# Second batch's exponentials taken slot by slot from PSUM on ScalarE, and wider zeros in the empty products

## The chip, the cores and the metric

The kernel runs on 1 core of one Trainium2 chip. The metric is the device time of one execution in microseconds (us); of several runs the median is given. PE is TensorE (PEld its weight loads), DVE is VectorE, ACT is ScalarE, POOL is GpSimd, SP is SyncE, which here issues DMAs.

## What is computed

Attention over two batches of 8 heads, 576 positions and head size 64. The first four heads see a local window of 32, the last four see every 32nd position. The result goes through a product of two linear maps, two more linear maps, and a mixture of four experts.

```python
scores = scale * np.matmul(q, k.transpose(0, 1, 3, 2))
...
scores = np.where(masks[None, :, :, :], scores, -1000000000.0)
scores = scores - np.max(scores, axis=-1, keepdims=True)
attn = np.exp(scores)
attn = attn / (np.sum(attn, axis=-1, keepdims=True) + 1e-09)
return np.matmul(attn, v).astype(np.float32)
...
a = x @ w1
b = x @ w2
h = a * b @ w3
return (h @ w_out).astype(np.float32)
...
p = domain_probs / (domain_probs.sum(-1, keepdims=True) + 1e-09)
for e in range(E):
    h = np.maximum(x @ w1[e], 0.0)
    out += p[:, e:e + 1] * (h @ w2[e])
```

Only masked-in blocks of the scores are computed. A slot is one such block: 64 columns for a local head, 54 for a strided one.

## The kernel before

**Stages.** Up to about 31 us the attention of the first batch (b = 0) runs alone, while the first weights arrive. From 31 us TensorE works on `x @ w1` and `x @ w2` (`ab_block`, accumulators `ab_acc`), in units of two accumulators, 12 matmuls of 288 columns each; after units 2, 4, 5, 7, 8, 10, 11, 13 and 14 one step of the second batch's attention (`attend(1, s)`, s = 0 to 8) is put between them. This lasts to about 98 us. Then follow the second batch's units, the map `w3 @ w_out`, its product with the former result, and the experts, to the end.

**Everything in full precision is done with split numbers.** A value is kept as a rounded part (`w_hi`, `x_hi`) and a remainder (`w_lo`, `x_lo`), and each product is three (`mm3`, L266 to L268). Making the parts is work for ACT and DVE: for each 1 MB piece of weights ACT runs L143, L151 and the rounding L172, and DVE runs L154, L157, L160, L164 and the remainder L182. `advance()` issues this work piece by piece between the units, so it stands on the same two queues as the attention.

**A step of the attention.** `Chunk4` holds 6 slots (local, g = 0) or 8 (strided, g = 1), six chunks for a batch. `scores` fills one PSUM bank `sc`. `maxima` reduces it to one maximum for each slot (L370) and writes score minus maximum to the tile `p_ring` (L375). `exps` is one ACTIVATE over all slots (L381). One step later `sums` adds up each slot (L390 or L388), adds 1e-9 (L391, g = 0 only; for g = 1 a column of 1e-9 that POOL has written is summed too) and inverts (L392), and `normalise` multiplies (L396, on POOL for b = 0, on DVE for b = 1). Then TensorE transposes (`tp`, L401), ACT copies the result out of PSUM (`pT`, L406), TensorE multiplies with the values (`o`, L418 or L427), ACT takes the rounded part (`x_hi`, L454) and DVE the remainder (`x_lo`, L458).

**Order.** Each engine works off its own instructions in the order in which the code issues them; semaphores make it wait for others. In `attend` that is: scores of s + 1, maxima and exps of s, sums and normalise of s - 1, product with values and rounding of s - 3, transposes and copy of s - 2. So on ACT the copy `pT`, the rounding `x_hi` and the copies `ab` that free TensorE's banks (L503) stand behind the exponentials of the same step. The accumulators `tp`, `o` and `ab_acc` share five PSUM banks (pool `ps`), the scores have three of their own.

**Empty products.** `keep_warm(n)` issues n products of zeros into a spare bank while TensorE would wait. There are 42 in the first 31 us, each 128x512 in bf16 with its own weight load (L119).

Of the kernel before, what the change touches and what calls it, by code (L numbers as in the profile page):

```python
# [8 lines left out]
F32 = mybir.dt.float32  # L9
F32R = mybir.dt.float32r  # L10
BF16 = mybir.dt.bfloat16
I32 = mybir.dt.int32
U32 = mybir.dt.uint32
AF = mybir.ActivationFunctionType
# [4 lines left out]
P = 128  # L19
# [9 lines left out]
NBLK = NT // BLK  # L29
NTT = NT // P  # L30
NEG = -8.0e9
WARM = 7
SCALE = 1.0 / float(D) ** 0.5

EXP_LO, EXP_HI = 3.0517578125e-05, 122880.0
# [7 lines left out]
def kernel(  # L43
# [13 lines left out]
    nc = tc.nc  # L57
    mm = nc.tensor.matmul
# [7 lines left out]
    small = ctx.enter_context(tc.tile_pool(name="small", bufs=4))  # L66
# [5 lines left out]
    def bank(name):  # L72
        return ps.tile([P, 512], F32, tag="ps", name=name)
# [33 lines left out]
    def warm_up():  # L107

        idle = tmp.tile([P, P], F32, tag="pT", name="idle")
        nc.vector.memset(idle, 0.0)  # L110
        nc.scalar.activation(small.tile([P, 1], F32, tag="rec", name="one"), idle[:, :1], AF.Exp)
        zeros = idle.bitcast(BF16)
        moving = zeros.unsqueeze(1).to_broadcast([P, 2, 2 * P])

        def keep_warm(n):
            if n:
                acc = bank("idle")
            for i in range(n):
                mm(acc.rearrange("p (a b) -> p a b", a=2), zeros[:, :P], moving, start=i == 0, stop=i == n - 1)  # L119

        keep_warm(WARM)
        return keep_warm
# [80 lines left out]
    def load_next(held=False):  # L203
        nonlocal loaded
        if loaded < len(stream):
            stream[loaded].raw_load(held)
            loaded += 1
            for load in rest_loads.pop(loaded, ()):
                load()
# [46 lines left out]
    def advance(n=1):  # L256

        return all([next(worker, False) for _ in range(n)])
# [16 lines left out]
    def load_qk(b, g, cut=0, held=False):  # L275

        pair = big[b].tile([P, 2, 2, S], F32, tag="big", name="tqk")
        tq, tk = pair[:, 0], pair[:, 1]
        hold(held, tk[:, 0, :1])
        pairs = slice(2 * g, 2 * g + 2)  # L280
        for c in ([slice(0, cut), slice(cut, S)] if cut else [slice(0, S)]):
            for t, src, queue in ((tk, kT, nc.sync), (tq, qT, nc.scalar if cut else nc.sync)):
                queue.dma_start(out=t[:, :, c], in_=src[b, pairs, :, c].rearrange("k p n -> p k n"))
        qk[b, g] = (tq, tk)
# [36 lines left out]
    class Chunk4:  # L321
# [45 lines left out]
        def maxima(self):  # L367
            s = self.slots
            mx = small.tile([P, 8], F32, tag="mx", name="mx")
            nc.vector.tensor_reduce(out=mx[:, :s], in_=self.sc, axis=mybir.AxisListType.X, op=ALU.max)  # L370
            self.frame = p_ring[self.index % 4]
            self.p = self.frame[:, :s, :self.nk]
            if self.g:
                nc.gpsimd.memset(self.frame[:, :, T3:T3 + 1], 1e-9)
            nc.vector.tensor_tensor(out=self.p, in0=self.sc, in1=self.wide(mx), op=ALU.subtract)  # L375
# [2 lines left out]
            return t[:, :self.slots].unsqueeze(2).to_broadcast([P, self.slots, self.nk])  # L378

        def exps(self):  # L380
            nc.scalar.activation(self.p, self.p, AF.Exp, scale=SCALE)  # L381

        def sums(self):
            s = self.slots
            self.rec = small.tile([P, 8], F32, tag="rec", name="rec")
            rec = self.rec[:, :s]
            if self.g:
                nc.vector.tensor_reduce(out=rec, in_=self.frame[:, :s, :T3 + 1], axis=mybir.AxisListType.X, op=ALU.add)  # L388
            else:
                nc.vector.tensor_reduce(out=rec, in_=self.p, axis=mybir.AxisListType.X, op=ALU.add)  # L390
                nc.vector.tensor_scalar_add(rec, rec, 1e-9)  # L391
            nc.vector.reciprocal(rec, rec)  # L392
# [188 lines left out]
    class Weights:  # L581
# [17 lines left out]
        def work(self):  # L599
# [20 lines left out]
            if self.again:  # L620
                for i, u in enumerate(sums):
                    nc.sync.dma_start(out=u.bitcast(F32), in_=stored[self.at][i])
            else:
                yield from self.split(sums, w)
                for i, u in enumerate(sums):
                    nc.sync.dma_start(out=stored[self.at][i], in_=u.bitcast(F32))
# [120 lines left out]

    with tc.manual_schedule():
        keep_warm = warm_up()
        load_qk(0, 0, CUT)  # L750
        local_masks()
# [63 lines left out]
        first[1].scores()  # L815
        for s in range(9):
            if s == 2:
                keep_warm(6)
                first[3].scores()
            if s == 3:  # L820
                keep_warm(2)
            if 3 <= s:
                first[s - 3].pv()
            if 2 <= s < 8:
                first[s - 2].transposes()
            if s + 1 in (2, 4, 5):
                first[s + 1].scores()
            keep_warm({0: 3, 5: 5, 6: 7, 7: 7, 8: 5}.get(s, 0))
            if s < 6:
                first[s].maxima()  # L830
                first[s].exps()
            if 1 <= s < 7:
                first[s - 1].sums()
                first[s - 1].normalise()
            if s in (3, 4, 6):
                load_next(True)
            if s == 5:
                load_qk(1, 0, held=True)
            if 3 <= s:
                first[s - 3].put()  # L840
                first[s - 3].put_lo()
                if s != 6:
                    live -= 1
            advance({5: 3, 6: 1, 7: 1}.get(s, 0))
            if 2 <= s < 8:
                first[s - 2].evac(nc.scalar.copy)
            if s == 6:
                c_w12[0].round_up()
# [21 lines left out]
        for it in range(8):  # L870
# [8 lines left out]
            i = {1: 0, 3: 1, 6: 2}.get(it)  # L879
# [141 lines left out]
```

## Time and profile before

| | us |
|---|---|
| median of 3 runs | 626.93 (626.92 to 627.87) |
| the profiled execution, its own time | 628.45 |
| its span, first to last instruction | 626.3 |
| PE busy | 615.6 |
| DVE busy | 450.4 |
| ACT busy | 265.0 |
| POOL busy | 10.1 |

The span is what the trace shows; the rest of the execution's own time lies around it. TensorE is busy for 98% of the span, so a wait of TensorE anywhere is a good part of what can be lost or won. A matmul's busy time includes its way through the array, so a few hundred ns of waiting can hide in it: start times tell more than busy shares.

### The profile page before, as it was taken

To read this page: it belongs to the slowest core of one execution; us is meant where nothing else is said; L and a number is where in the kernel's file an instruction comes from. 1 tells how busy PE (TensorE), PEld (TensorE's weight loads), DVE (VectorE), ACT (ScalarE), POOL (GpSimd) and SP (SyncE) were. 2 spreads that over 40 slices of the span, in tenths; PEclk is the share of its full clock that TensorE was granted. 3 is DMA by queue.
4 is the path that set the end of the run, shared out by engine and by line. 5 is a ranking of instruction groups with operands and counts; after the bars stand their busy time and mean duration, and the time that the engine had idled before them with its cause. 6 is when DMAs were issued, how large, how long until landed. Compare 5 with 4: busy or idle time off the path is not lost.

```text
span 626.3 us, 11330 instructions
## 1 busy us (share of the span) xinstructions
PE 615.6 (98%) x4632; PEld 559.5 (89%) x4632; DVE 450.4 (72%) x813; ACT 265.0 (42%) x455; POOL 10.1 (2%) x37
## 2 busy tenths in 40 slices
PE   8899999999999999999999999999999999999997
PEld 5598899999889999999989999899889898989996
DVE  4889995989784224867977888788775665755843
ACT  3564574765654123433343433434433333333320
POOL 4100000000000000000000000000000000000000
PEclk9899999999999999999999999999999999999999
DMA  8876330235522210344344344354586566565411
GB/s 262 291 272 190 127 137 2 92 124 186 205 78 97 95 68 1 135 163 174 135 166 170 136 173 163 135 188 159 196 297 253 181 224 219 186 214 189 154 49 67
DMA packets 28726, 99.43 MB, mean 159 GB/s; under 512 B 2652, under 2 KB 6740, under 8 KB 26116
## 3 DMA queue, kind: packets, MB, share of 16 engines
q1 hardware_dynamic: 28132, 98.14, 44.5%
q8 instruction: 36, 0.59, 0.4%
q10 hardware_dynamic: 544, 0.59, 0.3%
q14 instruction: 14, 0.11, 0.1%
HBM read 79.58 MB, written 19.14 MB: 158 GB/s over the span
## 4 chain that ended last, share of the span: by engine, by line
PE 88%; DVE 4%; DMA 3%; ACT 3%; issue 2%; POOL 0%; SPq 0%; DVEq 0%
PE g_acc L266 11%; PE g_acc L267 11%; PE g_acc L268 10%; PE m_a L268 4%; PE m_a L267 4%; PE m_a L266 4%; PE m_b L267 3%; PE m_c L266 3%; PE x_acc L268 3%; PE x_acc L267 3%; PE x_acc L266 3%; PE m_c L267 3%; PE m_b L266 3%; PE m_c L268 3%; PE m_b L268 3%; PE ab_acc L266 3%
## 5 line engine op out<-in xcount | busy, mean ns | idle before, releaser
L657 ACT ACTIVATE h_hi<-u 128x320 fp32r<-128x320 f32 (+1 forms) x128 | 56.9, 445 | 189.0 <-DVE u L663 189.0
L266 PE MATMUL g_acc<-w_hi,h_hi 128*128 128x512 f32 (+1 forms) x296 | 114.3, 386 | 0.0
L267 PE MATMUL g_acc<-w_lo,h_hi 128*128 128x512 f32 (+1 forms) x296 | 114.2, 386 | 0.0
L268 PE MATMUL g_acc<-w_hi,h_lo 128*128 128x512 f32 (+1 forms) x296 | 113.7, 384 | 0.0
L596 DVE TENSOR_TENSOR w_lo<-raw,w_hi 128x768 fp32r<-128x768 f32 x64 | 69.4, 1084 | 12.4 <-ACT w_hi L594 12.4
L663 DVE TENSOR_TENSOR u<-m_b,u 128x320 f32<-128x320 f32 (+1 forms) x96 | 40.7, 452 | 51.1 <-PE m_b L268 51.1
L266 PE MATMUL ab_acc<-x_hi,w_hi 128*128 128x288 f32 x252 | 75.2, 298 | 1.3 <-ACT pT L406 1.0
L268 PE MATMUL ab_acc<-x_hi,w_lo 128*128 128x288 f32 x252 | 74.2, 294 | 0.0
L267 PE MATMUL ab_acc<-x_lo,w_hi 128*128 128x288 f32 x252 | 74.2, 294 | 0.0
L268 PEld LDWEIGHTS g_acc<-w_hi,h_lo 128*128 128x128 f32 x296 | 55.6, 188 | 11.6
L266 PEld LDWEIGHTS g_acc<-w_hi,h_hi 128*128 128x128 f32 x296 | 55.8, 188 | 8.0
L267 PEld LDWEIGHTS g_acc<-w_lo,h_hi 128*128 128x128 f32 x296 | 55.7, 188 | 7.6
L659 DVE SCALAR_TENSOR_TENSOR h_lo<-u,h_hi 128x320 fp32r<-128x320 f32 (+1 forms) x128 | 57.6, 450 | 3.6 <-ACT h_hi L657 1.8
L594 ACT CAST w_hi<-raw 128x768 fp32r<-128x768 f32 x64 | 59.9, 936 | 0.0
L266 PEld LDWEIGHTS ab_acc<-x_hi,w_hi 128*128 128x128 f32 x252 | 47.3, 188 | 2.0 <-ACT pT L406 1.2
L267 PEld LDWEIGHTS ab_acc<-x_lo,w_hi 128*128 128x128 f32 x252 | 47.3, 188 | 0.0
L268 PEld LDWEIGHTS ab_acc<-x_hi,w_lo 128*128 128x128 f32 x252 | 47.3, 188 | 0.0
L267 PE MATMUL m_b<-b_t,s_hi 128*128 128x320 f32 (+1 forms) x128 | 37.9, 296 | 0.0
L663 DVE TENSOR_TENSOR u<-m_a,u 128x320 f32<-128x320 f32 (+1 forms) x64 | 28.9, 451 | 11.6 <-PE m_a L268 11.6
L596 DVE TENSOR_TENSOR s_lo<-raw,s_hi 128x1024 fp32r<-128x1024 f32 x16 | 19.6, 1225 | 24.3 <-ACT s_hi L594 24.3
L663 DVE TENSOR_TENSOR u<-m_c,u 128x320 f32<-128x320 f32 (+1 forms) x64 | 29.0, 452 | 4.5 <-PE m_c L268 3.9
L673 ACT COPY u<-m_a 128x320 f32<-128x320 f32 (+1 forms) x32 | 12.7, 398 | 42.3 <-PE m_a L268 42.3
(162 smaller groups left out, 1398.2 us busy)
## 6 DMA issues: line engine op xcount, KB each, us to landing
raw<-in_e_dram SPq DMA_DIRECT2D x32, 1024.0 KB, 5.1
raw<-in_w_dram SPq DMA_DIRECT2D x8, 1024.0 KB, 6.4
raw<-in_w3T_dram SPq DMA_DIRECT2D x8, 1024.0 KB, 4.9
stored<-s_hi SPq DMA_DIRECT2D x16, 512.0 KB, 2.6
stored<-s_lo SPq DMA_DIRECT2D x16, 512.0 KB, 2.6
s_hi<-stored SPq DMA_DIRECT2D x16, 512.0 KB, 3.5
s_lo<-stored SPq DMA_DIRECT2D x16, 512.0 KB, 6.9
raw<-in_w_out_dram SPq DMA_DIRECT2D x4, 1024.0 KB, 8.4
```

Of the source, the lines that this page charges most:

```text
L266: mm(acc, lh, rh, start=first, stop=False)
L267: mm(acc, lh, rl, start=False, stop=False)
L268: mm(acc, ll, rh, start=False, stop=last)
L594: nc.scalar.copy(dst[0], src)
L596: nc.vector.tensor_tensor(out=dst[1], in0=src, in1=dst[0].bitcast(F32), op=ALU.subtract)
L657: nc.scalar.activation(hi, src, AF.Relu)
L659: nc.vector.scalar_tensor_tensor(out=lo, in0=src, scalar=0.0, in1=hi.bitcast(F32), op0=ALU.max, op1=ALU.subtract)
L663: nc.vector.tensor_tensor(out=out, in0=acc, in1=b, op=ALU.add)
L673: nc.scalar.copy(u1, a)
```

## The change

In the second batch (b = 1) `maxima` keeps only the reduction; POOL multiplies the maxima by -SCALE. `exps` becomes one ACTIVATE for each slot: it reads the scores from PSUM, takes the scaled maximum as its bias, and writes the sum of its slot (`accum_out`) to `rec`. `sums` shrinks to an addition of 1e-9, on POOL, and the reciprocal on DVE. `keep_warm` multiplies 32-bit zeros, 128x512, instead of bf16, and is called for 10 products instead of 42: 2 for 7 at the start, 1 for 6, 0 for 2, 1 for 3, 1 for 5, 2 for 7 twice, 1 for 5.

```diff
-WARM = 7
+WARM = 2
...
-        zeros = idle.bitcast(BF16)
-        moving = zeros.unsqueeze(1).to_broadcast([P, 2, 2 * P])
+        moving = idle.unsqueeze(1).to_broadcast([P, 4, P])
...
-                mm(acc.rearrange("p (a b) -> p a b", a=2), zeros[:, :P], moving, start=i == 0, stop=i == n - 1)
+                mm(acc.rearrange("p (a b) -> p a b", a=4), idle, moving, start=i == 0, stop=i == n - 1)
...
             self.p = self.frame[:, :s, :self.nk]
+            if self.b:
+                self.mx = mx
+                nc.gpsimd.tensor_scalar_mul(mx[:, :s], mx[:, :s], -SCALE)
+                return
             if self.g:
                 nc.gpsimd.memset(self.frame[:, :, T3:T3 + 1], 1e-9)
             nc.vector.tensor_tensor(out=self.p, in0=self.sc, in1=self.wide(mx), op=ALU.subtract)
...
         def exps(self):
+            if self.b:
+                self.rec = small.tile([P, 8], F32, tag="rec", name="rec")
+                for s in range(self.slots):
+                    at = slice(s, s + 1)
+                    nc.scalar.activation(self.p[:, s], self.sc[:, s], AF.Exp, bias=self.mx[:, at], scale=SCALE,
+                                         accum_out=self.rec[:, at])
+                return
             nc.scalar.activation(self.p, self.p, AF.Exp, scale=SCALE)
...
-            self.rec = small.tile([P, 8], F32, tag="rec", name="rec")
+            if not self.b:
+                self.rec = small.tile([P, 8], F32, tag="rec", name="rec")
             rec = self.rec[:, :s]
-            if self.g:
+            if self.b:
+                nc.gpsimd.tensor_scalar_add(rec, rec, 1e-9)
+            elif self.g:
...
             if s == 2:
-                keep_warm(6)
+                keep_warm(1)
                 first[3].scores()
-            if s == 3:
-                keep_warm(2)
...
-            keep_warm({0: 3, 5: 5, 6: 7, 7: 7, 8: 5}.get(s, 0))
+            keep_warm({0: 1, 5: 1, 6: 2, 7: 2, 8: 1}.get(s, 0))
```

Line numbers in the changed kernel differ by a few: exponentials L381 become L388, maxima L370 become L369, `x_lo` L458 becomes L471.

On DVE, step s = 1 of the second batch stands like this before; `t` and `w_lo` belong to the splitting of weights, `mx` are the maxima, `rec` the sums and their inverses.

```order
L164 ISA t<-raw_621,t 128x2048
L370 TENSOR_REDUCE mx<-sc 128x6
L375 TENSOR_TENSOR p_ring<-sc,mx 128x384
L390 TENSOR_REDUCE rec<-p_ring 128x6
L391 TENSOR_SCALAR rec<-rec 128x6
L392 RECIPROCAL rec<-rec 128x6
L396 TENSOR_TENSOR p_ring<-p_ring,rec 128x384
L154 TENSOR_SCALAR t<-t 128x1024
```

And in the changed kernel, at the same place on DVE:

```order
L163 ISA t<-raw_592,t 128x2048
L369 TENSOR_REDUCE mx<-sc 128x6
L405 RECIPROCAL rec<-rec 128x6
L409 TENSOR_TENSOR p_ring<-p_ring,rec 128x384
L153 TENSOR_SCALAR t<-t 128x1024
```

The subtraction, the sum and the addition have left DVE's row; the reciprocal stands right behind the maxima, and in front of it, on POOL, now stand the scaling of this step's maxima and the addition to the last step's sums, in that order.

On ACT, step s = 3 stands like this before; `x_hi` and `pT` are the attention's, `ab` frees a bank of TensorE, `raw` and `t` are weights.

```order
L381 ACTIVATE p_ring<-p_ring 128x8x54
L454 CAST x_hi<-o 128x2x3x32 x2
L406 COPY pT<-tp 128x384
L503 COPY ab<-ab_acc 128x288
L143 ACTIVATE raw_883<-raw_883 128x1024
```

And in the changed kernel, at the same place on ACT:

```order
L388 ACTIVATE p_ring,rec<-sc,mx 128x54 x8
L467 CAST x_hi<-o 128x2x3x32 x2
L419 COPY pT<-tp 128x384
L516 COPY ab<-ab_acc 128x288
L142 ACTIVATE raw_856<-raw_856 128x1024
```

One exponential has become eight, and the same rounding, copies and weight work stand behind them in the same order.

## Rows read from the trace of the kernel before

**Rows 1.** The page: busy us (share) xinstructions; the chain's shares by engine.

```profile
PE 615.6 (98%) x4632; PEld 559.5 (89%) x4632; DVE 450.4 (72%) x813; ACT 265.0 (42%) x455; POOL 10.1 (2%) x37
...
PE 88%; DVE 4%; DMA 3%; ACT 3%; issue 2%; POOL 0%; SPq 0%; DVEq 0%
```

**Rows 2.** Busy time by stretch: us, PE, PEld, DVE, ACT, POOL, clock, DMA.

```profile
50.00:70.00 20.00, 19.14 (x300) 17.93 (x300) 19.41 (x36) 10.14 (x17) 0.23 (x2) 1.00 0.62 204
```

**Rows 3.** Waits of PE from 30 to 190 us, the longest: total us, times, longest.

```profile
PE ab_acc L266 <- ACT pT L406: 1.0, 1, 1.0
```

**Rows 4.** The chain that ended last, step 0: start us, us, what.

```profile
43.91 0.53 ACT p_ring L381
...
44.72 0.95 ACT w_hi L172
```

**Rows 5.** Timeline of DVE, 42 to 72 us: start us, us, engine, line, operation [idle before].

```profile
42.73 0.55 DVE L370 TENSOR_REDUCE mx<-sc 128x6 f32<-128x384 f32 x1
...
45.70 1.23 DVE L182 TENSOR_TENSOR w_lo<-t,w_hi 128x1024 fp32r<-128x1024 f32 x1 [0.49 <-ACT w_hi L172]
...
53.71 1.21 DVE L182 TENSOR_TENSOR w_lo<-t,w_hi 128x1024 fp32r<-128x1024 f32 x1
...
69.37 0.60 DVE L370 TENSOR_REDUCE mx<-sc 128x8 f32<-128x432 f32 x1
...
71.93 0.61 DVE L458 TENSOR_TENSOR x_lo<-o,x_hi 128x192 fp32r<-128x192 f32 x2
```

**Rows 6.** Timeline of ACT, 44 to 81 us.

```profile
44.34 0.38 ACT L503 COPY ab<-ab_acc 128x288 f32<-128x288 f32 x1
...
52.09 1.05 ACT L172 CAST w_hi<-t 128x1024 fp32r<-128x1024 f32 x1
...
60.74 1.05 ACT L172 CAST w_hi<-t 128x1024 fp32r<-128x1024 f32 x1 [0.54 <-DVE t L164]
...
71.12 0.52 ACT L454 CAST x_hi<-o 128x192 fp32r<-128x192 f32 x2
...
80.08 0.60 ACT L406 COPY pT<-tp 128x512 f32<-128x512 f32 x1
```

**Rows 7.** Timeline of PE, step 5.

```profile
80.73 0.83 PE L427 MATMUL o<-pT,tv_str 54*64 54x54 f32 x32 [0.62 <-ACT pT L406]
```

**Rows 8.** ACT's groups by form: line, operation, shapes xcount | busy us, mean ns.

```profile
L381 ACT ACTIVATE p_ring<-p_ring 128x432 f32<-128x432 f32 x6 | 3.4, 566 | 12.7 <-DVE p_ring L375 12.7
L381 ACT ACTIVATE p_ring<-p_ring 128x384 f32<-128x384 f32 x6 | 3.1, 524 | 17.7 <-DVE p_ring L375 17.7
L454 ACT CAST x_hi<-o 128x192 fp32r<-128x192 f32 x12 | 3.1, 313 | 0.1
L111 ACT ACTIVATE one<-idle 128x1 f32<-128x1 f32 x1 | 0.2, 202 | 0.0
```

**Rows 9.** POOL's groups by form, its smallest.

```profile
L374 POOL MEMSET p_ring<- 128x8 f32 x6 | 0.7, 114 | 35.5 <-PE tp L401 35.5
...
L86 POOL TENSOR_SCALAR_AFFINE_SELECT m_str<-m_str 128x54 bf16<-128x54 bf16 x2 | 0.5, 244 | 0.1
```

**Rows 10.** Timeline of all engines, 25 to 30 us, first batch's last chunk.

```profile
25.27 0.20 DVE L392 RECIPROCAL rec<-rec 128x8 f32<-128x8 f32 x1
...
25.61 0.92 POOL L396 TENSOR_TENSOR p_ring<-p_ring,rec 128x432 f32<-128x432 f32 x1 [2.90 <-DVE rec L392]
...
26.59 0.66 PE L401 MATMUL tp<-ident,p_ring 128*128 128x128 f32 x4 [0.16 <-POOL p_ring L374]
...
27.08 1.67 PE L119 MATMUL idle<-idle 128*128 128x512 bf16 x7
...
29.52 0.66 ACT L454 CAST x_hi<-o 128x108 fp32r<-128x108 f32 x4 [1.60 <-PE o L427]
```

**Rows 11.** Busy time by stretch, two microseconds of the first batch (columns as in rows 2).

```profile
17.00:18.00 1.00, 0.20 (x10) 0.09 (x6) 0.88 (x3) 0.98 (x4) 0.12 (x1) 1.00 0.91 385
...
19.00:20.00 1.00, 1.00 (x43) 1.00 (x42) 0.39 (x1) 0.00 (x0) 0.00 (x0) 0.50 0.93 164
```

## The prediction, made before the changed kernel ran

> **What bounds the kernel now.** I read the page first: TensorE is busy 98% of the span, and the chain that ended last runs over PE for 88% of it [rows 1]. So the kernel gets longer by what TensorE waits more, and shorter by what it waits less. The busy time by stretch comes next. From 50 to 70 us, where the second batch's attention lies between the first products, DVE is busy 19.41 of 20 us, PE 19.14 and ACT 10.14 [rows 2]. By shares DVE is full and ACT is half empty, which is what the change goes by. But shares don't say who is waited for, so I read the waits and then the timelines of one step after the other. TensorE's longest wait there is for ACT's copy `pT` [rows 3]. In step 0 the chain goes through ACT: the exponential at 43.91, then the rounding `w_hi` at 44.72 [rows 4], and DVE stands idle 0.49 us until that rounding is done [rows 5]. In step 5 TensorE waits 0.62 us for `pT` [rows 7]. ACT's exponentials stand in front of all of these in its queue. So ACT, half idle, is in the loop that sets the pace: DVE's maxima, ACT's exponentials, ACT's `w_hi`, `x_hi` and `pT`, then DVE's remainders and the next maxima, or TensorE.
>
> **The change, part 1: what leaves DVE.** For each of six chunks the subtraction and the sum go, and in the first three the small addition. Each costs about as much as the maxima beside it, 0.55 us for 6 slots and 0.60 for 8 [rows 5], so some 1.2 us a chunk, 7 us in all. Taken alone this would shorten DVE's queue. Against it stands a new wait: DVE's reciprocal follows the maxima of the same step, and waits for POOL, which first scales these maxima and then adds 1e-9. Queued behind the waiting reciprocal are DVE's multiplication and the weights, and ACT's `w_hi` waits for those.
>
> **Part 2: the way over POOL.** The trace has no such POOL operation. The nearest rows are a fill of 128x8, 0.11 us, and a select of 128x54, 0.24 us [rows 9]; I take 0.20, nearer to the second because it reads its operand too. From DVE's end to POOL's start it is 0.14 us (25.47 to 25.61), and from POOL's end to TensorE's start 0.06 (26.53 to 26.59) [rows 10], which I also take for POOL to ACT. So from the end of the maxima to ACT's first exponential: 0.14 + 0.20 + 0.06 = 0.40 us (ends 0.31 and 0.44). DVE's reciprocal starts 0.60 us after the maxima, a second POOL operation later. That is 3.0 us over five steps, so DVE still gains some 4 us, if anything waits for it.
>
> **Part 3: the exponentials.** Now 42 ACTIVATEs do what 6 did. One over 384 elements takes 524 ns, one over 432 takes 566 [rows 8]: 0.875 ns an element, so 64 columns alone would be 524 - 320 x 0.875 = 244 ns and 54 columns 235. ACT starts the next instruction 0.10 us before a record ends (43.91 + 0.53 = 44.44 [rows 4] against 44.34 [rows 6]), which leaves 0.144 and 0.135 us a slot. That is the low end, with bias and sum free. Neither a bias read from memory nor a sum written out is in the trace. The smallest ACT operation, one element a partition, records 202 ns [rows 8], or 0.10 us with the overlap off. I take one such step for fetching the bias and one for writing the sum: 0.344 us a slot in a local chunk, 0.335 in a strided one. The high end, overlap lost and a whole 0.20 for the sum, is about 0.45.
>
> The Trainium skill, "ScalarE: Activation LUTs", What ACT_TABLE_LOAD costs, gives an ACTIVATE with a bias from memory as about 280 ns + 0.833 ns an element, overlapping the next by about 93 ns; by that alone an estimate for 64 columns is 0.24 us, and it has no price for the sum. No run here shows it yet; as a result of its own it is the first rival below.
>
> **Part 4: step by step.** I measure from the end of the maxima to the start of the next ACT instruction that others wait for. Before, local: 43.28 [rows 5] to 44.34 [rows 6], 1.06 us; strided: 69.97 [rows 5] to 71.12 [rows 6], 1.15. After, local: 0.40 + 6 x 0.344 = 2.46, so 1.40 later; strided: 0.40 + 8 x 0.335 = 3.08, so 1.93 later. What of it reaches the path is that less the slack which ACT's results have today:
> - step 0: none, since DVE waits 0.49 us for `w_hi` [rows 5]: +1.40.
> - step 1: `w_hi` ends at 53.14 [rows 6], DVE takes it up at 53.71 [rows 5]: 0.57 slack, +0.83.
> - step 2: `w_hi` stood ready 0.54 us before its input came [rows 6]: +0.86.
> - steps 3 and 4: `x_hi` starts at 71.12 [rows 6], the first of two ends 0.31 later [rows 8], and DVE reads it at 71.93 [rows 5]: 0.50 slack in step 4, taken for step 3 too: +1.43 each.
> - step 5: `pT` ends at 80.68 [rows 6], TensorE starts at 80.73 [rows 7]: no slack, +1.93.
>
> Sum 7.9 us. It adds up because each step's maxima stand behind DVE work that waits for the step before. DVE's 4 us of relief don't count here: in each of these steps DVE would wait for ACT. Nor does anything later hide the delay: behind this stretch TensorE is the engine that others wait for.
>
> **Part 5: the empty products.** Most lie where TensorE waits anyway; the path runs through the last seven (27.08) [rows 10], since the product with values behind them ends the wait of `x_hi` at 29.52 [rows 10]. Seven in bf16 took 1.67 us, 0.24 each. No row has a 32-bit product of this size. Four transposes of 128 columns in 32 bits start at 26.59 and the next work at 27.08 [rows 10], which by column would make 0.49 us of 512; four times the bf16 price would make 0.95. I take the second, as the products aren't transposes: two cost 1.9 us, 0.2 more than seven did; at the other end they would cost 0.7 less. So +0.2, from -0.7. The clock is the risk: from 17 to 18 us TensorE was busy 0.20 us, and from 19 to 20 the granted clock was 0.50, the 1.2 GHz level [rows 11]. Fewer products in other places can move or lengthen such a stretch; I allow 1 us either way.
>
> **Sum.** 7.9 + 0.2 = 8.1 us. The profiled execution took 628.45 us for a span of 626.3; with the change I expect 636.6 and a span of 634.4. The median of the runs is 1.5 us below the profiled execution, so the time to forecast is 626.9 + 8.1 = 635.0.
>
> **Rivals.**
> - **The sum rides free (630.8).** If only the bias costs a step, a slot is 0.10 us cheaper, 4.2 us over 42 slots. For it: the adder may work while elements stream. Against it: a second result has to get into memory. The price of the Trainium skill's page named above comes out at the same place.
> - **Slots are cheap, and DVE's relief shows (625.5, faster).** At 0.144 and 0.135 us a slot ACT is only 0.2 us later in a local step and 0.33 in a strided one, less than the slack in steps 1 to 4. Then DVE's lighter queue counts, and TensorE gets back its 1.0 us [rows 3] and part of 0.62 [rows 7], together about 1.5. It decides at some 0.17 us a slot. For it: DVE is at 97% and ACT at 51% from 50 to 70 us [rows 2]. Against it: bias and sum would both have to be free.
> - **Worse than forecast (639.5).** At 0.45 us a slot, 0.11 x 42 = 4.6 us more. Or the clock falls: TensorE would wait 2 to 3 us at a time in steps 3 to 5, longer than the pause before the drop to 0.50 [rows 11], and a half unit of products takes twice as long at 1.2 GHz.
> - **Only the empty products count (627.1).** If the exponentials were hidden altogether, what is left is the +0.2. Nothing in the timelines speaks for it, as step 5 has no slack.
>
> **How the numbers follow.** Forecast 0.52 (633 to 638), free sum 0.18, worse 0.17, cheap slots 0.08, only the empty products 0.05. The range goes from 629.5, a slot of 0.21, to 640. A measurement here can tell 0.2%, 1.25 us: faster means under 625.7, and slower over 628.2. Faster 0.08, same 0.05, slower 0.87.
>
> **What would show it.** In the changed profile the L388 group has 42 ACTIVATEs; their spacing in a step is the price that decides (0.34 here; under 0.17 and I am wrong on the sign). DVE should show idle time before `x_lo` (L471) and the reciprocal (L405) where it was full; TensorE should wait 2 to 3 us for `x_hi`, `x_lo` or `pT` in steps 3 to 5, and from 100 us on all should look as before, about 8 us later. If the wait for POOL is far over 0.6 us, part 2 is wrong; if the first full product starts at other than 31.3 us, part 5 is.

## The result, and the profile after

The changed kernel takes 635.03 us (median of 4 runs, 634.03 to 636.24) against 627.4 for the kernel before in the same comparison (626.92 to 628.23). The ratio is 1.0118, 95% interval 1.0099 to 1.0137, so it is 7.6 us slower. The profiled execution took 634.89 us, its span is 633.1. Executions of one kernel mostly differ by 1 to 3 us, and in some of them TensorE's clock falls for a few microseconds, in the first batch or the second.

I read the page as in [rows 1] first: the busy line, the 40 slices and the chain of the changed kernel.

```profile
PE 618.1 (98%) x4610; PEld 561.0 (89%) x4610; DVE 444.3 (70%) x798; ACT 274.5 (43%) x533; POOL 13.1 (2%) x46
...
PE   8899889999999999999999999999999999999997
...
PEclk9999889999999999999999999999999999999999
...
PE 82%; issue 5%; DVE 5%; ACT 4%; DMA 3%; POOL 1%; POOLq 0%; SPq 0%; DVEq 0%; ACTq 0%
```

DVE has 6 us less to do and ACT 9.5 more; the span is 6.8 us longer all the same, and TensorE has lost share of the chain. Two dents in the second row, slices 5 and 6, are about 63 to 95 us: the second batch's strided steps. The stretches around them, the first as in [rows 2] (columns: us, PE, PEld, DVE, ACT, POOL, clock, DMA):

```profile
50.00:70.00 20.00, 16.16 (x277) 14.76 (x276) 14.29 (x24) 13.33 (x53) 1.46 (x6) 1.00 0.55 191
70.00:90.00 20.00, 17.14 (x174) 16.41 (x174) 14.78 (x28) 14.18 (x52) 1.22 (x5) 0.84 0.16 54
```

From 50 to 70 us DVE fell from 19.41 to 14.29 us, and PE with it, from 19.14 to 16.16. ACT is at 67%, no engine is full: all wait for one another. Nearly the whole loss is made ahead of 100 us. From the last product of `ab_block` ahead of a wait near 150 us to the end it is 480.2 us before and 480.1 after.

One step on ACT, to be held against [rows 6] (start us, us, engine, line, operation, idle before and releaser), the first strided chunk:

```profile
65.69 0.31 ACT L388 ACTIVATE p_ring<-sc,mx 128x54 f32<-128x54 f32 x1 [2.75 <-POOL mx L374]
65.89 0.19 ACT L388 ACTIVATION_READ_ACCUMULATOR p_ring<-sc,mx 128x1 f32 x1
65.98 0.30 ACT L388 ACTIVATE p_ring<-sc,mx 128x54 f32<-128x54 f32 x1
...
67.67 0.34 ACT L388 ACTIVATE p_ring<-sc,mx 128x54 f32<-128x54 f32 x1
67.85 0.24 ACT L388 ACTIVATION_READ_ACCUMULATOR p_ring<-sc,mx 128x1 f32 x1
67.94 0.57 ACT L467 CAST x_hi<-o 128x192 fp32r<-128x192 f32 x2
68.35 0.55 ACT L419 COPY pT<-tp 128x384 f32<-128x384 f32 x1
```

A slot is two records, an ACTIVATE and a read of the accumulator. From slot to slot it is 0.28 us here and 0.29 in the local chunks, 2.25 us for eight. ACT stood idle 2.75 us ahead of them; then `x_hi` and `pT` wait for all eight. The same stretch on DVE, which answers to [rows 5], and on TensorE, which answers to [rows 3]:

```profile
64.72 0.60 DVE L369 TENSOR_REDUCE mx<-sc 128x8 f32<-128x432 f32 x1
66.01 0.19 DVE L405 RECIPROCAL rec<-rec 128x6 f32<-128x6 f32 x1 [0.69 <-POOL rec L399]
66.23 0.56 DVE L409 TENSOR_TENSOR p_ring<-p_ring,rec 128x384 f32<-128x384 f32 x1
68.33 0.62 DVE L471 TENSOR_TENSOR x_lo<-o,x_hi 128x192 fp32r<-128x192 f32 x2 [1.54 <-ACT x_hi L467]
```

```profile
65.65 0.91 PE L363 MATMUL sc<-tqk 64*18 64x18 f32 x32
68.95 0.90 PE L431 MATMUL o<-pT,tv_loc 64*64 64x32 f32 x48 [2.40 <-ACT pT L419]
...
83.34 0.29 PE L267 MATMUL ab_acc<-x_hi,w_lo 128*128 128x288 f32 x1
85.94 0.79 PE L440 MATMUL o<-pT,tv_str 54*64 54x54 f32 x32 [2.31 <-ACT pT L419]
```

DVE, lighter by the subtraction and the sum, waits 0.69 us for POOL and 1.54 us for `x_hi`. TensorE waits 2.40 and 2.31 us for `pT`, where the longest waits for it were 1.0 and 0.62 us [rows 3, 7].

Behind each of these two waits the clock falls to 0.50, the 1.2 GHz level (two microseconds a row, clock third from the end; [rows 11] are rows of the same view):

```profile
68.00:70.00 2.00, 1.05 (x49) 1.01 (x50) 1.67 (x3) 2.00 (x7) 0.00 (x0) 0.95 0.04 16
70.00:72.00 2.00, 2.00 (x10) 2.00 (x10) 2.00 (x4) 1.32 (x2) 0.00 (x0) 0.50 0.00 0
...
84.00:86.00 2.00, 0.06 (x2) 0.06 (x3) 0.78 (x3) 2.00 (x12) 0.23 (x1) 1.00 0.82 348
86.00:88.00 2.00, 2.00 (x39) 1.94 (x40) 1.63 (x3) 2.00 (x7) 0.00 (x0) 0.72 0.03 8
88.00:90.00 2.00, 2.00 (x10) 2.00 (x9) 1.97 (x6) 0.43 (x2) 0.00 (x0) 0.50 0.00 0
```

From 88 to 90 us ten products run, against 17 in the same two microseconds of the softmax-only kernel below, whose clock stayed full.

### The profile page after: what moved, and what is told of

Read it like the earlier page. It is cut to its first block, busy times and chain, and to the rows that moved or that the text cites. A ratio compares the mean times of both kernels' runs of the same rounds, so it can differ in the third digit from the quotient of the medians.

```text
span 633.1 us, 11356 instructions
## 1 busy us (share of the span) xinstructions
PE 618.1 (98%) x4610; PEld 561.0 (89%) x4610; DVE 444.3 (70%) x798; ACT 274.5 (43%) x533; POOL 13.1 (2%) x46
## 3 DMA queue, kind: packets, MB, share of 16 engines
HBM read 79.58 MB, written 19.14 MB: 156 GB/s over the span
## 4 chain that ended last, share of the span: by engine, by line
PE 82%; issue 5%; DVE 5%; ACT 4%; DMA 3%; POOL 1%; POOLq 0%; SPq 0%; DVEq 0%; ACTq 0%
PE g_acc L265 10%; PE g_acc L266 10%; PE g_acc L267 10%; PE m_a L267 4%; PE m_a L266 4%; PE m_a L265 4%; PE m_b L266 3%; PE m_c L265 3%; PE x_acc L267 3%; PE x_acc L266 3%; PE x_acc L265 3%; PE m_c L266 3%; PE m_b L265 3%; PE m_c L267 3%; PE m_b L267 3%
## 5 line engine op out<-in xcount | busy, mean ns | idle before, releaser
L265 PE MATMUL ab_acc<-x_hi,w_hi 128*128 128x288 f32 x252 | 76.7, 304 | 1.5 <-ACT ab L516 1.0
L265 PEld LDWEIGHTS ab_acc<-x_hi,w_hi 128*128 128x128 f32 x252 | 48.6, 193 | 2.6 <-ACT ab L516 1.4
```

The lines of the kernel that those rows point to most:

```text
L265: mm(acc, lh, rh, start=first, stop=False)
```

## The experiments

To compare traces whose first 31 us differ, I measure one stretch in each: from the first product of the first unit to the product of `ab_block` named above. Here its two ends are in the kernel before and after.

```profile
31.10 0.79 PE L498 MATMUL ab_acc<-x_hi,w_hi 128*128 128x288 f32 x4 [0.43 <-ACT w_hi L172]
...
146.01 0.29 PE L268 MATMUL ab_acc<-x_hi,w_lo 128*128 128x288 f32 x1
```

```profile
29.77 0.80 PE L511 MATMUL ab_acc<-x_hi,w_hi 128*128 128x288 f32 x4 [0.56 <-ACT w_hi L171]
...
152.96 0.29 PE L267 MATMUL ab_acc<-x_hi,w_lo 128*128 128x288 f32 x1
```

That is 114.91 us before and 123.19 after, 8.28 more. Three numbers of each kernel stand in this table; the ratio is against the kernel before in the same comparison, the stretch is from the one profiled execution. From the end of the stretch to the end of the span it is 480.1 to 480.9 us in all rows but two: 483.3 in "before, exponential last", where the clock fell there too, and 479.8 in "long waits filled".

| kernel | median us | ratio to before, 95% | stretch against before, us |
|---|---|---|---|
| the change | 635.03 | 1.0099 to 1.0137 | +8.28, clock fell |
| softmax only | 633.54 | 1.0090 to 1.0125 | +6.52, clock full |
| empty products only | 627.81 | 0.9992 to 1.0009 | 0.00 |
| no sum | 630.97 | 1.0045 to 1.0078 | +2.98, clock full |
| scale and 1e-9 on DVE | 632.73 | 1.0071 to 1.0097 | +5.68, clock fell |
| exponentials last | 630.03 | 1.0023 to 1.0055 | +2.66, clock full |
| slots spread | 625.23 | 0.9941 to 0.9974 | -1.49, clock full |
| local chunks only | 629.06 | 1.0011 to 1.0031 | +2.00, clock full |
| strided chunks only | 634.35 | 1.0078 to 1.0118 | +7.05, clock fell |
| before, exponential last | 626.92 | 0.9972 to 1.0008 | +0.98, clock fell |
| spread, scale and 1e-9 on DVE | 623.89 | 0.9919 to 0.9955 | -3.42, clock full |
| waits filled, wrong steps | 634.69 | 1.0086 to 1.0122 | +7.75, clock fell |
| long waits filled | 635.31 | 1.0105 to 1.0139 | +9.82, clock fell |

**The two halves of the change.** The first kernel is the changed one with the 42 empty products of before (its diff against the change is below, cut); the second is the kernel before with the ten 32-bit products alone.

```diff
-WARM = 2
+WARM = 7
...
-        moving = idle.unsqueeze(1).to_broadcast([P, 4, P])
+        zeros = idle.bitcast(BF16)
+        moving = zeros.unsqueeze(1).to_broadcast([P, 2, 2 * P])
...
-            keep_warm({0: 1, 5: 1, 6: 2, 7: 2, 8: 1}.get(s, 0))
+            keep_warm({0: 3, 5: 5, 6: 7, 7: 7, 8: 5}.get(s, 0))
```

> The changed kernel with the 42 bf16 empty products of before. Theory: the changed softmax costs all of the loss, and the new empty products give 1.3 us back in the first 31 us. Then the first product of the first unit starts at about 31.1 us as before, not at 29.8, and the time is 635.0 + 1.3 = 636.3 us. Rival: the empty products only move a wait that comes back later; then 635.0 us, as with the whole change. Second rival: they also decide how TensorE's clock stands in the second batch's steps; then the half-clock stretches at 70 and 88 us are gone and the time is under 635.

> The kernel before with the ten 32-bit empty products alone. Theory: the 1.3 us that the first batch is shorter in the changed profile come from them: first unit at about 29.8 us, 627.2 - 1.3 = 625.9 us. Rival, as forecast: the last two cost what seven did or 0.2 us more, and the time stays at 627.2 to 627.5. In this rival the 1.3 us are scatter of that one profile or come from the shorter program of the new softmax.

Measured: 633.54 us (633.02 to 636.19) and 627.81. The theory that the empty products give 1.3 us back fell; with them alone nothing changes. The stretch after them is the same to 0.01 us, and the early start in the profile of the change is the first batch's clock: the first unit starts at 31.1 to 31.5 us in the four profiles whose clock up to 31 us is 0.94 (before, exponentials last, local only and long waits filled), and at 29.6 to 30.8 in all others, with 32-bit products or bf16 ones on either side. So the softmax makes the loss: its interval, 1.0090 to 1.0125, holds the change's 1.0118. Its profiled execution kept the clock at 1.00 and shows the loss without a fall: 6.52 us. The runs of this kernel at a mean clock of 1.000 took 633.0 and 633.4 us, those at 0.994 to 0.997 took 633.5 to 636.2. The empty products alone don't decide on that: lower mean clocks come with either kind.

**The price of a slot.**

```diff
-                    nc.scalar.activation(self.p[:, s], self.sc[:, s], AF.Exp, bias=self.mx[:, at], scale=SCALE,
-                                         accum_out=self.rec[:, at])
+                    nc.scalar.activation(self.p[:, s], self.sc[:, s], AF.Exp, bias=self.mx[:, at], scale=SCALE)
...
-                nc.gpsimd.tensor_scalar_add(rec, rec, 1e-9)
+                nc.gpsimd.tensor_scalar_add(rec, self.mx[:, :s], 1e-9)
```

> The changed kernel without the sum output of the 42 exponentials; the division is by the scaled maximum instead of the sum, with the same POOL and DVE instructions. Theory: the 213 ns read record behind each exponential goes, and with it 0.09 us of the 0.29 us from slot to slot: 42 x 0.09 = 3.8 us less, nothing of it hidden: 631.2 us. Rival: the ACTIVATE itself becomes the pace (0.24 us or more a slot without the read), 42 x 0.05 = 2 us less: 633. Second rival: the slots' price is hidden beside other work, 635 as before the edit.

Measured: 630.97 us, as the theory had it (the kernel leaves out the sum, so what it computes is no longer the attention). ACT in one local step:

```profile
56.69 1.34 ACT L388 ACTIVATE p_ring<-sc,mx 128x64 f32<-128x64 f32 x6 [2.69 <-POOL mx L374]
57.89 0.51 ACT L418 COPY pT<-tp 128x384 f32<-128x384 f32 x1
```

Six slots from 56.69 to 57.89: 0.20 us each without the sum, 0.29 with it. The stretch is 3.54 us shorter than with the sum (2.98 against 6.52); 42 x 0.09 is 3.8.

**The way over POOL.**

```diff
-                nc.gpsimd.tensor_scalar_mul(mx[:, :s], mx[:, :s], -SCALE)
+                nc.vector.tensor_scalar_mul(mx[:, :s], mx[:, :s], -SCALE)
...
-                nc.gpsimd.tensor_scalar_add(rec, rec, 1e-9)
+                nc.vector.tensor_scalar_add(rec, rec, 1e-9)
```

> The changed kernel with the multiplication by the scale and the addition of 1e-9 on DVE, not on POOL. Theory: the way over POOL is paid on the path: from the maxima to the first exponential about 0.2 us instead of 0.36 to 0.44 (0.75 in step 0), so 5 x 0.2 + 0.5 = 1.5 us less: 633.5 us. Rival: DVE's wait of 0.7 us for POOL in front of the reciprocal is what costs, five times 0.5 us more: 631. Second rival: DVE waits later for ACT in any case, and nothing of it shows: 635.

Measured: 632.73 us, 2.3 less than the change. From the maxima to the first exponential it is now 0.24 to 0.25 us (0.30 in step 0). That accounts for some 1.2 us. The clock fell in this profile too, so the rest is not told apart. DVE's wait for POOL is gone, and in its place DVE waits 1.7 to 1.8 us for `x_hi`, where it waited 1.4 to 1.5: relief of DVE alone goes into the next wait for ACT.

**Do the steps add up?** The new softmax for the three local chunks alone, then for the three strided ones alone. The condition below replaces `self.b` in four places; the strided kernel has `self.b and self.g`.

```diff
-            if self.b:
+            if self.b and not self.g:
```

> Only the three local chunks of the second batch go slot by slot; the strided ones are as before. Theory: the costs of the steps add up, each by its own slots less its own slack. With the measured 0.29 us a slot: step 0 (0.40 + 6 x 0.29) - 1.06 = 1.08, and 0.35 for the long first POOL operation; steps 1 and 2 1.08 less 0.57 and 0.54. Together 2.5 us: 630 us. Rival: in the local steps DVE's relief takes most of it back, and the loss lies in the strided steps: 628.

> Only the three strided chunks of the second batch go slot by slot; the local ones are as before. Theory: 0.42 + 8 x 0.283 = 2.68, less 1.15 of before: 1.53 later a step, less 0.50 slack in steps 3 and 4 and none in step 5: 3.6 us, 631 us, and half a microsecond to two more where TensorE's clock falls after a wait. Rival: the loss isn't the sum of its steps; one long wait in step 5 sets it and the rest is hidden: 629.

Measured: 629.06 and 634.35 us. In the stretch the local chunks cost 2.00 us. The strided ones cost 7.05, but up to their last wait only 3.92 (products with values of the first strided chunk at 83.29, 53.55 us into the stretch; before, 80.73 [rows 7], 49.63). At the end of that wait the clock fell to 0.50:

```profile
82.00:84.00 2.00, 0.71 (x26) 0.72 (x30) 1.44 (x4) 2.00 (x8) 0.23 (x1) 0.75 0.63 266
84.00:86.00 2.00, 2.00 (x25) 1.90 (x20) 1.63 (x3) 1.75 (x6) 0.00 (x0) 0.50 0.03 8
86.00:88.00 2.00, 2.00 (x11) 2.00 (x10) 1.97 (x7) 0.22 (x1) 0.00 (x0) 0.50 0.00 0
```

So the waits are 2.0 + 3.9 = 5.9 us in two parts against 6.5 in one; the steps add up within 0.6 us. The expected 2.5 and 3.6 were right to 0.5.

**Is it ACT's time, or what stands behind it?** First the exponentials at the end of the step, then cut up into pieces of at most three slots and spread over the half units.

```diff
                 chunk[s].maxima()
-                chunk[s].exps()
...
                 chunk[s - 2].evac(nc.scalar.copy)
+            if s < n:
+                chunk[s].exps()
```

> The changed kernel with the exponentials of a step issued after the rounding x_hi and the copy pT of the same step, so that on ACT these stand ahead of them. Theory: the slots cost nothing by themselves, since ACT is idle up to 2.7 us in each step; they cost because ready copies stand behind them. Then the waits of 2.3 to 2.4 us for pT and x_lo in steps 3 to 5 go, 5.6 of the 6.5 us that the changed softmax costs; what stays is the ab copies and w_hi behind them in steps 0 to 2. About 629.5 us. Rival: ACT's work as such is too much or w_hi and the ab copies now wait as long instead: 633 to 635.

```diff
                 next(block)
                 advance(1)
+                if late:
+                    c, slots = late.pop(0)
+                    c.exps(slots)
...
                 chunk[s].maxima()
-                chunk[s].exps()
...
                 chunk[s - 2].evac(nc.scalar.copy)
+            if s < n:
+                c, m = chunk[s], chunk[s].slots
+                c.exps(range(0, 2))
+                late.extend((c, range(i, min(i + 3, m))) for i in range(2, m, 3))
```

> The changed kernel with the slots cut up: two at the end of the step, then two or three at a time behind each half unit, so that no copy stands behind more than three slots, 0.9 us. Theory: then nearly all of the 6.5 us goes, and DVE's relief of 4 us can show: 627 to 628.5 us, the time of before or slightly over. Rival: the price is ACT's time itself, 42 x 0.29 = 12 us in place of 3, wherever it stands: 633 or more.

Measured: 630.03 us, and 625.23, which is under the kernel before. This settles it: the spread slots cost ACT as many records and no less time (14.1 us in all, 12.9 in the changed kernel), and nothing is lost. With the exponentials merely last, TensorE still waits 1.53 us for `x_lo` at its first strided products with values. ACT and DVE in the spread kernel, in the same step as above:

```profile
63.08 0.31 ACT L389 ACTIVATE p_ring<-sc,mx 128x54 f32<-128x54 f32 x1 [1.92 <-POOL mx L374]
...
63.66 0.40 ACT L517 COPY ab<-ab_acc 128x288 f32<-128x288 f32 x1
63.94 0.33 ACT L389 ACTIVATE p_ring<-sc,mx 128x54 f32<-128x54 f32 x1
```

```profile
64.10 0.61 DVE L472 TENSOR_TENSOR x_lo<-o,x_hi 128x192 fp32r<-128x192 f32 x2
```

The copy `ab` runs behind two slots; `x_hi` and `pT` had run ahead of them, and `x_lo` follows DVE's multiplication without a wait. From 50 to 70 us, in the spread kernel:

```profile
50.00:70.00 20.00, 19.45 (x307) 18.68 (x304) 16.43 (x30) 16.75 (x63) 1.89 (x8) 1.00 0.56 192
```

ACT does even more in this stretch than in the changed kernel, 16.75 us, and TensorE is busy 19.45.

**What of this gain is the order, what DVE's relief?** The kernel before with its one exponential at the end of the step (the same diff as for "exponentials last"), and the spread slots with POOL's two operations on DVE.

> The kernel before with the exponential of a step issued after x_hi and pT of the same step, nothing else. If the order alone is what the spread slots gained by, TensorE's waits for pT of 1.0 and 0.6 us in steps 4 and 5 go: 626.0 us. If DVE's relief is what the spread slots gained by (DVE is 97% busy from 50 to 70 us in the kernel before), the order alone gives nothing: 627.6. A third outcome: the copies that now stand ahead of the exponential wait themselves for TensorE, and the exponential is late for the next step: over 628.

> The spread slots with the multiplication by the scale and the addition of 1e-9 on DVE. Theory: where nothing on TensorE's way waits for the maxima any more, the way over POOL costs nothing: 625.2 us as with the spread slots. Rival: DVE's waits for POOL, 0.7 us five times, still stand ahead of the weights' parts; without them 0.5 to 1.5 us less: 624 us.

Measured: 626.92 us (ratio 0.9972 to 1.0008, no difference that can be told; two of its 11 runs took 632 us at a clock of 0.992 and 0.995, and the profile is of one of them), and 623.89. The trace says more of the order alone than the median does. Up to the product that stands behind the wait of 1.0 us for `pT` before [rows 3], it is 1.59 us shorter than before, and the spread slots are 1.92. In the next step it loses this again:

```profile
78.86 0.56 ACT L381 ACTIVATE p_ring<-p_ring 128x432 f32<-128x432 f32 x1 [2.45 <-DVE p_ring L375]
79.33 0.38 ACT L503 COPY ab<-ab_acc 128x288 f32<-128x288 f32 x1
```

```profile
79.77 0.67 PE L427 MATMUL o<-pT,tv_str 54*64 54x54 f32 x28 [1.21 <-ACT ab L503]
```

The exponential of step 5 waits 2.45 us for DVE's subtraction, the copy `ab` stands behind it, TensorE waits 1.21 us for the bank that `ab` frees, and the clock falls behind that. In the spread kernel DVE has no subtraction, and the wait at this place is 0.37 us. So in this profile the order alone brings most of the gain up to step 4, and what it runs into in step 5 is DVE's work. How much of the rest is DVE's relief and how much the smaller pieces was not told apart: no run has one without the other. The second kernel shows that the way over POOL counts with the order mended too: in the spread kernel DVE waited 0.7 to 0.8 us for POOL five times; without that the stretch is 1.93 us shorter and the median 1.3, though the two intervals overlap a little. Part of it may be the way to the first exponential, 0.24 us here where it was 0.36 to 0.43. I had expected no change here, so that was a miss. The kernel with spread slots and no POOL is 0.63% faster than before.

**The clock.** Two kernels put empty products into the long waits. The first stood in the wrong steps, one call of `attend` early. The second, whose diff is below, put them ahead of the products that wait; `fill` issues two 32-bit products.

```diff
             banks = [bank("o") for _ in range(2)]
+            if self.b and self.index in (1, 3):
+                fill(banks[0])
...
             run_unit()
+            if done == 9:
+                fill(ps_sc.tile([P, 512], F32, tag="sc", name="sc"))
```

> The changed kernel with two more 32-bit empty products in steps 3 and 5, right ahead of the products with values that wait 2.4 us for pT; what they write is not used. They put 1.8 us of work into either wait. Theory: the granted clock falls to 0.50 after these waits in most executions, and the last fall costs 1.8 us; with the waits filled it stays at 1.00 in all, and the time is 633.2 us, with little scatter. Rival: the fall has nothing to do with the waits, or the empty products delay what follows; 635 us or more.

> The changed kernel with two 32-bit empty products, 1.8 us, in each of the three waits of TensorE that are longer than 2 us: ahead of the products with values of the second and the fourth chunk, written into the bank that these products then overwrite, and behind the ninth unit, into a free bank of the scores. Theory: the falls of the clock to 0.50 come behind these waits; filled, the clock stays at 1.00 in every execution, and the time is that of the executions without a fall, 633.0 to 633.5 us, with a scatter under 1 us. Rival: the falls are only a small part of the loss in most executions, or have another cause: 634.5 to 635 us as without the filling. Second rival: the filling makes TensorE late where the wait is shorter than it: over 635.5.

Measured: 634.69 and 635.31 us, no gain; neither shows what makes the clock fall. In the second it stayed at 1.000 in three of four runs, in the change in none of four (0.994 to 0.999), too few to show a cause. The second shows something else:

```profile
67.00 0.91 PE L368 MATMUL sc<-tqk 64*18 64x18 f32 x32
70.10 3.60 PE L323 MATMUL o<-ident 128*128 128x512 f32 x4 [2.19 <-DVE x_lo L478]
```

The empty products, which need no `pT`, wait as well, for the bank that DVE's `x_lo` frees. Then they run after the wait, here at half clock, and delay the rest. So the wait put down to `pT` is one for `x_lo` too; in the changed kernel `x_lo` ends at 68.95, just when the products start. Both stand behind the same exponentials. The runs of this kernel at full clock took 634.9 to 635.3 us, the one at 0.995 took 637.4.

## Why the prediction was right, and where two errors cancelled

The forecast was 635.0 and the median is 635.03. The mechanism is the one named, but the hit is closer than its terms were. As a loss it is 7.6 us against 8.1, since the kernel before took 627.4 in this comparison and not 626.9. And the 7.6 hold falls of the clock, which the sum left out: where the clock was 1.000, the softmax-only kernel took 633.0 and 633.4 us.

- **The bound.** Right: the exponentials stand in front of `w_hi`, `x_hi`, `pT` and `ab` in ACT's queue. Moving or spreading them takes 5 to 10 us away with the same number of slots, which excludes ACT's time as such.
- **Part 1, DVE.** Right that the relief doesn't count in this order: DVE waits for ACT up to 1.54 us a time. The wait for POOL was put at 0.60 us after the maxima, and DVE waits 0.68 to 0.82 us, 3.6 in all.
- **Part 2, POOL.** Said 0.40 us from the maxima to the first exponential; it is 0.36 to 0.44 in five steps, and 0.75 in step 0, which was not foreseen (last section).
- **Part 3, the slot. This is the mis-sized term.** The sum costs 0.09 us, said 0.10. But a slot without the sum takes 0.20, where 0.144 bare and a whole step of 0.10 for the bias made 0.244: bare slot and bias together were priced too high, and no run separates the two. 0.29 and 0.28 in place of 0.344 and 0.335 are 2.2 us less over 42 slots. By the Trainium skill, "ScalarE: Activation LUTs", What ACT_TABLE_LOAD costs, the estimate without the sum was 0.24 us. The trace has 0.20, with records of 322 ns where that page makes 333. It doesn't quite agree, and the measurement decides.
- **Part 4, step by step.** Measured from the maxima's end to the next ACT instruction: 2.50, 2.11, 2.11 in the local steps (said 2.46), 2.62, 2.70, 2.68 in the strided (said 3.08). With the measured slots and the 0.35 of step 0 the sum of the steps becomes 7.9 - 2.2 + 0.35 = 6.05 us; the stretch without a fall shows 6.52. So slacks and adding up held to half a microsecond.
- **Part 5, empty products.** A 32-bit product takes 0.905 us (two start 1.81 us apart from what follows), said 0.95. They change nothing that can be measured, said +0.2; the microsecond either way that was allowed for the clock is what the profiles show. By the prediction's own sign, a first full product at 31.3 us, this part was wrong for the profiled execution: it starts at 29.77 (see the span, below).
- **The clock. Not in the sum, only in a rival.** TensorE waited 2.3 to 2.4 us, and in the profiled execution the clock fell twice. The first fall cost nothing, since a shorter wait absorbed it: the product that waits for `x_lo` starts 45.84 us into the stretch with the fall and 45.85 without it. It waits 0.55 us in the changed kernel and 2.11 in the softmax-only one:

```profile
75.60 0.40 PE L265 MATMUL ab_acc<-x_hi,w_hi 128*128 128x288 f32 x1 [0.55 <-DVE x_lo L471]
```

```profile
75.46 0.40 PE L266 MATMUL ab_acc<-x_hi,w_hi 128*128 128x288 f32 x1 [2.11 <-DVE x_lo L472]
```

  The second fall had no wait behind it and cost 1.8 us (67.02 against 65.24 us from the products at 85.94 to the end of the stretch, in the softmax-only kernel those at 85.80). This put back most of the 2.2 us that the slots had been overpriced by, which is luck.
- **The span.** Forecast 634.4, found 633.1: the forecast started from a profile of before whose first unit began at 31.10, and the changed one began at 29.77. The difference goes with the half-clock stretch of [rows 11], which this profile of after doesn't have: all four profiles with such a stretch start their first unit at 31.1 us or later, all ten without it at 30.8 or earlier.
- **The rivals.** "The sum rides free" fell: without the sum the time is 4 us shorter. "Slots are cheap" put the turning point at 0.17 us a slot; at 0.20 the kernel is still 3.4 us slower than before. "Worse than forecast" had the right second half, the clock. "Only the empty products count" fell: with them alone the time is that of before.

## What to carry to other kernels

Work moved to an engine that is half idle is not free if it goes in front of short copies that others wait for: price the delay of what stands behind it, step by step, not the engine's busy share. The same work issued behind those copies, in pieces of at most three, turned 7.6 us of loss into 2.4 of gain. Before a hit is taken as proof, measure each term alone; here two errors of about 2 us had cancelled.

## What the runs showed of the hardware that I had not expected

- An exponential with a sum shows as two records, and the read of 213 ns costs 0.09 us of ACT's time, since it overlaps its neighbours.
- A small POOL operation (128 x 6) takes 0.24 us, but 0.63 in step 0:

```profile
42.02 0.63 POOL L374 TENSOR_SCALAR mx<-mx 128x6 f32<-128x6 f32 x1 [16.99 <-DVE mx L369]
...
50.97 0.24 POOL L374 TENSOR_SCALAR mx<-mx 128x6 f32<-128x6 f32 x1 [8.33 <-DVE mx L369]
```

```profile
41.84 0.68 DVE L153 TENSOR_SCALAR t<-t 128x1024 f32<-128x1024 f32 x1
```

  It runs beside a DVE operation with one scalar and ends 0.13 us after it. It is not that this is POOL's first operation of the kind: where only the strided chunks were changed, the first took 0.25 us beside a reduction (DVE L403, 62.71 to 63.25). In the spread kernel another took 0.76 us from 80.22, beside the like DVE operation L156 (80.20 to 80.89). By the Trainium skill, "SBUF — State Buffer", Who interferes with whom, such a DVE operation can hold the ports that it shares with GpSimd for its whole length. These three cases agree; no run here took the DVE operation away from step 0.
- Why TensorE's clock fell was not found. It fell to 0.50, the 1.2 GHz level, at or just behind waits of 1.2 to 2.4 us in the second batch of six profiles, and stayed at 1.00 through waits as long in others: the change and the softmax-only kernel have the same two waits for `pT` (2.40 and 2.31 us, 2.42 and 2.29), and only the first shows falls there.
